# Loads held back until the pooled keys are transposed, and some weight forms on GpSimd, in a pooled-attention and mixture kernel

## The chip, the cores and the metric

The kernel runs on one core of a Trainium2 chip. The metric is the device time of one execution in microseconds; three executions of the kernel before gave 528.2, 528.27 and 527.43, median 528.2. The profiled execution has a span of 526.9 us.

## The reference

Attention with pooled keys and values, followed by a mixture of four two-layer experts:

```python
k_p = k.reshape(B, H, Sp, 8, D).mean(axis=3)        # 576 keys -> 72
v_p = v.reshape(B, H, Sp, 8, D).mean(axis=3)
attn = softmax(q @ k_p.T / sqrt(D))                 # B = 8, H = 8, S = 576, D = 64
x = (attn @ v_p) as [B * S, H * D]                  # 4608 x 512
out = sum over e of p[:, e] * (relu(x @ w1[e]) @ w2[e])   # 4 experts, 512 -> 1024 -> 512
```

with `p` the domain probabilities divided by their sum. All inputs are float32 and are loaded as bf16; the result is float32.

## The kernel before

The tokens are worked in nine chunks of 512: chunk c < 8 holds the first 512 tokens of batch c, and chunk 8 the 64 remaining tokens of all eight batches. A step is one (chunk, expert) pair, 36 in all. In step s TensorE computes the hidden layer of step s and, between its products, the second layer of step s - 1. Most steps multiply by a seven-product scheme (Strassen's, with sums formed ahead of time): `up_seven` and `up_down` form the hidden layer from seven products of 2 x 2 blocks, each accumulated in PSUM; the blocks are sums of halves of x (`forms_of`, tiles `xf`), of w1 (`combine_w1`, written into spare parts of `w1_bf`), of w2 for experts 1 and 2 (`combine_w2`, tile `w2_t`) and of the hidden layer (`sums_of`, tile `h_s`). Chunk 0 is computed in the plain way, and so is the first expert of chunk 1 (`up_plain`); from then on the forms of the weights have to be there.

The attention of batch b = c + 1 is woven into the four steps of chunk c. This is written out by hand: a chunk's plan is a dictionary from a point number to pieces of work, and each pass through `between` or `slot` moves to the next point. In the plan of chunk c, entry n stands at the (2n + 1)st point after the chunk's start, so n runs from 0 to 31, eight to a step. Besides the plan there is a queue `forms_due` of weight and x forms: each `slot` takes one of them, then the pieces of the point. All engines run their own instructions in the order in which the program issues them; between engines only data and buffers hold them.

The pieces of one batch's attention, with their entries before for c > 1:

- `key_parts`: VectorE folds the eight keys of a pool, in two halves of the heads, from the tile `raw` into `kp` (L205, L210, L213).
- `keys` (entry 1; 3 in chunk 1): the SP queue transposes `kp` into `kpT` by DMA (L227).
- `load_v` (entry 2): POOL issues the load of v into the tile `raw` (L91), which holds one batch's k or v and is free once the keys are folded. For batches 1 and 2, v goes into the part of `w2_t` that the w2 forms take later. `load_q` and `load_q_rem` of the next batch come at the same entry (L108, L127).
- `scores` (entries 7 to 10): TensorE multiplies `kpT` and `qT` (L257), ScalarE exponentiates.
- `value_parts` (entries 8 to 11): VectorE folds v into `vp` in the same way (L205, L210, L213).
- `queries` and `load_k` of the next batch (entry 12): the SP queue transposes q (L240), POOL loads k (L91).
- `context` and `turn` (entries 11 to 15): TensorE multiplies exponentials and `vp` (L380), VectorE divides (L361, L362), the SP queue transposes the result into `xT` (L401).

The SP queue carries, in order, all DMA transposes and the output stores (L834). POOL does nothing but issue loads once its constants are made. POOL runs ahead of the others, so a load starts as soon as its buffer is free and the earlier loads of the queue are issued.

Of the kernel before, what the change touches and what calls it, by code (L numbers as in the profile page):

```python
# [13 lines left out]
BF16 = mybir.dt.bfloat16  # L14
# [4 lines left out]
def kernel(  # L19
# [10 lines left out]
    nc = tc.nc  # L30
# [18 lines left out]
    SPLIT = (1, 2)  # L49
# [4 lines left out]
    const = ctx.enter_context(tc.tile_pool(name="const", bufs=1))  # L54
# [124 lines left out]
    state = {}  # L179
# [45 lines left out]
    def keys(b):  # L225
        state[("kpT", b)] = apool.tile([P, H, SPP], BF16, name="kpT", bufs=3)
        nc.sync.dma_start_transpose(  # L227
            out=state[("kpT", b)][:], in_=kp[:].rearrange("j h u d -> j (h u d)")
        )

    def fold_values(b, hs):
        raw = raws[("vraw", b)]
        fold(raw, hs)
        nc.vector.tensor_add(
            out=vps[b % 3][:, hs, 0:D], in0=raw[:, hs, 0, :], in1=raw[:, hs, 1, :]
        )
# [226 lines left out]
    def rem_turn(i):  # L463
        flip(state.pop(("xr", i)), x_rem[:, :, i * P:(i + 1) * P])
# [56 lines left out]
    def attention(c):  # L521

        lo, hi = halves
        b = c + 1
        plan = {}

        def add(n, *what):
            plan.setdefault(n, []).extend(what)

        if c % 2:  # L530
            i = c // 2
            add(18, lambda: rem_queries(i))
            add(23, lambda: rem_scores(i))
            add(26, lambda: rem_context(i))
            add(27, lambda: rem_turn(i))
        if b == B:
            for part in forms_of(B):
                add(31, part)
            return plan
        if c == 1:  # L540
            keyed = 3
            add(0, lambda: queries(b))
            for n, part in enumerate(key_parts(b)):
                add(n, part)
        else:
            keyed = 1
            for n, part in enumerate(key_parts(b)[2:]):
                add(n, part)
        scored, valued, mixed = 7, 8, 11
        add(keyed, lambda: keys(b))  # L550
        if c > 1:
            add(keyed + 1, lambda: load_v(b))
        if b + 1 < B:
            add(keyed + 1, lambda: (load_q(b + 1), load_q_rem(b + 1)))
        for pair in range(NPAIR):
            add(scored + pair, lambda pair=pair: scores(b, pair))
        for n, part in enumerate(value_parts(b)):
            add(valued + n, part)
        if b + 1 < B:
            add(valued + 4, lambda: queries(b + 1), lambda: load_k(b + 1))  # L560
            for n, part in enumerate(key_parts(b + 1)[:2]):
                add(30 + n, part)
        for r in range(NR):
            add(mixed + r, lambda r=r: context(b, r))
            add(mixed + 1 + r, lambda r=r: turn(b, r))
        for n, part in enumerate(forms_of(b)):
            add((20, 21, 28, 29)[n], part)
        return plan
# [4 lines left out]
    A11, A12, A21, A22, S1, S2, S4 = range(7)  # L573
    S3 = A21

    def combine_w1(e):

        w = w1_bf[:, e]
        add, sub = nc.vector.tensor_add, nc.vector.tensor_sub
        return [  # L580
            lambda: add(out=w[:, S1], in0=w[:, A21], in1=w[:, A22]),
            lambda: sub(out=w[:, S2], in0=w[:, S1], in1=w[:, A11]),
            lambda: sub(out=w[:, S4], in0=w[:, A12], in1=w[:, S2]),
            lambda: sub(out=w[:, S3], in0=w[:, A11], in1=w[:, A21]),
        ]
# [21 lines left out]

    def combine_x(c):

        for part in forms_of(c):  # L610
            part()

    def combine_w2(e):

        lo, hi = slice(0, TH), slice(TH, DM)
        b11, b12 = w2_bf[:, e, 4:8, lo], w2_bf[:, e, 4:8, hi]
        b21, b22 = w2_bf[:, e, 0:4, lo], w2_bf[:, e, 0:4, hi]
        t1, t2, t4 = (w2_t[:, SPLIT.index(e), i] for i in range(3))
        sub = nc.vector.tensor_sub
        return [  # L620
            lambda: sub(out=t1, in0=b12, in1=b11),
            lambda: sub(out=t2, in0=b22, in1=t1),
            lambda: sub(out=b12, in0=b22, in1=b12),
            lambda: sub(out=t4, in0=b21, in1=t2),
        ]
# [217 lines left out]
    with tc.manual_schedule(engines={ENG.PE, ENG.DVE, ENG.Activation, ENG.Pool, ENG.SP}):  # L843
        nc.vector.memset(zeros[:], 0.0)
        nc.vector.memset(pool_map[:], 1.0)
        for vp in vps:
            nc.vector.memset(vp[:, :, D:D + 1], float(POOL))
        nc.vector.memset(kp[64:SPP], 0.0)
        for hs in halves:
            load_first(k, "k", hs)  # L850
        nc.gpsimd.affine_select(
            out=pool_map[:], in_=pool_map[:], compare_op=ALU.is_ge, fill=0.0,
            base=0, pattern=[[1, FT], [-POOL, SP]], channel_multiplier=FT,
        )
        nc.gpsimd.affine_select(
            out=pool_map[:], in_=pool_map[:], compare_op=ALU.is_ge, fill=0.0,
            base=POOL - 1, pattern=[[-1, FT], [POOL, SP]], channel_multiplier=-FT,
        )
        for half in range(2):
            load_first_q(half)  # L860
        make_identity(nc, ident[:])
        for hs in halves:
            load_first(v, "v", hs)
        load_w1(0)
        load_w2(0)
        attention_first()
        load_probs()
        load_w1(1)
        load_w1(2)
        load_w2(1)  # L870
        load_w1(3)
        load_k(1)
        load_w2(2)
        load_q(1)
        load_v(1)
        load_w2(3)
        load_q_rem(0)
        load_q_rem(1)

        steps = [(c, e) for c in range(NCH) for e in range(E)]  # L880
        forms_due = deque()
        placed = {}
        at = 0

        def point():
            nonlocal at
            for piece in placed.pop(at, ()):
                piece()
            at += 1

        def slot():
            if forms_due:
                forms_due.popleft()()
            point()

        for s in range(len(steps) + 1):
            live = s < len(steps)
            if live:
                c, e = steps[s]
                if e == 0:  # L900
                    plan = second_attention() if c == 0 else {}
                    if 0 < c < B:
                        plan = {at + 2 * n + 1: what for n, what in attention(c).items()}
                    for n, what in plan.items():
                        placed.setdefault(n, []).extend(what)

            def between(j, n):
                point()
                if s > 0:
                    down(*steps[s - 1], j, n)  # L910
                slot()

            nothing = [lambda: None] * 4
            if s == 1:
                forms_due.extend(nothing + combine_w1(2))
            elif s == 2:
                forms_due.extend(combine_w1(3))
            elif s == 4:
                forms_due.extend(combine_w1(1) + forms_of(1))
            elif s == 5:  # L920
                forms_due.extend(combine_w1(0) + combine_w2(SPLIT[0]) + combine_w2(SPLIT[1]))
            for j in range(2):
                if not live:
                    for n in range(4):
                        between(j, n)
                elif s == 0:
                    for i in range(4):
                        up_half(j, i)
                        if j == 0 and i in (1, 2):
                            turn_here(0, i + 1)  # L930
                        if j == 0 and i == 2:
                            norm_probs()
                            combine_x(0)
                        between(j, i)
                elif s == 1:
                    for n in range(4):
                        between(j, n)
                    for n in range(4):
                        up_plain(c, e, [4 * j + n])
                elif s == E:  # L940
                    for n in range(4):
                        between(j, n)
                        if j:
                            up_plain(c, e, [2 * n, 2 * n + 1])
                elif splits(*steps[s - 1]):
                    up_down(c, e, j, *steps[s - 1])
                else:
                    up_seven(c, e, j, lambda n: between(j, n))
# [30 lines left out]
```

The softmax here doesn't subtract the row's maximum and nothing guards it: scores larger than these inputs give would overflow.

## Time and profile before

| | busy us | share of the span |
|---|---|---|
| PE (matmul) | 506.4 | 96% |
| DVE (VectorE) | 353.0 | 67% |
| ACT (ScalarE) | 267.7 | 51% |
| POOL (GpSimd) | 46.8 | 9% |

| transfers by issue | count | median us to landing |
|---|---|---|
| kpT<-kp, DMA transpose on SP | 6 | 7.0 |
| qT<-q_sb, DMA transpose on SP | 6 | 4.3 |
| raw<-v, load on POOL, 576 KB | 5 | 10.0 |
| q_sb<-q, load on POOL, 512 KB | 7 | 13.5 |

PE is the engine that sets the end. Its idle time and its clock are therefore what counts; the other engines' busy time counts only where PE waits for them. In a line of waits the engine and line that waited stand ahead of the arrow, what ended the wait behind it, and then the total in us, the number of waits and the longest. In a timeline line stand the start, the time, the engine (with q for its queue), line, operation, out<-in and the number of instructions merged; in brackets is the idle time of the engine just before, with what ended it.

### The profile page before, as it was taken

The numbers are of one execution on the slowest core, as the hardware profiler recorded it, in microseconds if no ns is written. First come the engines' busy times: TensorE is split into PE (matmuls) and PEld (weight loads), VectorE is DVE, ScalarE is ACT, GpSimd is POOL, SyncE is SP. The second block draws the span as 40 slices with busy tenths as digits, with TensorE's granted clock in tenths as the row PEclk, the third lists the DMA queues.
The fourth block names the chain that finished last, engine by engine and source line by source line (L and its number), as shares of the span: only waits on it lengthen the run. The fifth ranks groups of instructions, "written<-read, shape, count | busy, mean of one in ns | idle before, by whom it ended". The sixth has DMA issues, their size and how long they took to land.

```text
span 526.9 us, 10142 instructions
## 1 busy us (share of the span) xinstructions
PE 506.4 (96%) x4171; PEld 365.0 (69%) x4171; DVE 353.0 (67%) x657; ACT 267.7 (51%) x467; POOL 46.8 (9%) x66
## 2 busy tenths in 40 slices
PE   8899986899999999999999999999999999999996
PEld 4656542468866885688668866887578768866883
DVE  2435786398867786678767876787687545764574
ACT  3554422645456554655366536554655445544650
POOL 8452101000010001000100010000000000000000
PEclk9899999899999999999999999999999999999999
DMA  9999999340089108830596049603320110011003
GB/s 137 206 206 205 196 150 150 76 80 1 12 157 133 20 1 139 132 49 11 92 155 63 2 78 159 82 12 50 90 40 1 41 52 1 12 40 40 1 1 80
DMA packets 75133, 41.56 MB, mean 79 GB/s; under 512 B 44480, under 2 KB 70464, under 8 KB 75088
## 3 DMA queue, kind: packets, MB, share of 16 engines
q0 software_dynamic: 33744, 22.63, 30.6%
q1 hardware_dynamic: 41344, 18.29, 17.8%
q8 instruction: 32, 0.52, 0.4%
q14 instruction: 13, 0.11, 0.1%
HBM read 45.16 MB, written 9.44 MB: 104 GB/s over the span
## 4 chain that ended last, share of the span: by engine, by line
PE 74%; DVE 11%; DMA 10%; issue 2%; POOL 2%; ACT 1%; DVEq 0%; POOLq 0%; ACTq 0%
PE g_ps L633 33%; PE o_ps L812 20%; PE u_ps L750 16%; DMA w_bf<-in_moe_w_dram 7%; DMA kpT<-kp 4%; DVE acc L756 2%; DVE H_sb L681 2%; PE two L257 2%; PE two L380 1%; DVE acc L826 1%; DVE h_s L696 1%; PE h_ps L651 1%; DVE x_tok L362 1%; POOL w_bf L142 1%; DVE xf L597 1%
## 5 line engine op out<-in xcount | busy, mean ns | idle before, releaser
L633 PEld LDWEIGHTS <-w_bf 128*128 128x128 bf16 x1848 | 176.2, 98 | 47.7 <-issue 9.2
L812 PE MATMUL o_ps<-w_bf,H_sb 128*128 128x512 bf16 x640 | 161.5, 379 | 0.0
L681 DVE CUSTOM_DVE_ANT_0 H_sb<-g_ps,r 128x512 bf16<-128x512 f32 x166 | 114.0, 687 | 65.1 <-ACT r L677 39.8
L633 PE MATMUL g_ps<-xf,w_bf 128*128 128x256 bf16 x1056 | 148.4, 272 | 2.2 <-DVE H_sb L681 1.2
L677 ACT COPY r<-g_ps 128x512 f32<-128x512 f32 x166 | 97.4, 587 | 102.6 <-PE g_ps L633 98.7
L756 DVE SCALAR_TENSOR_TENSOR acc<-u_ps,p_all,acc 128x512 f32<-128x512 f32 (+1 forms) x128 | 77.9, 612 | 44.0 <-ACT u_ps L776 43.3
L633 PE MATMUL g_ps<-xT,w_bf 128*128 128x256 bf16 x696 | 99.9, 273 | 0.3 <-DVE H_sb L681 0.3
L812 PEld LDWEIGHTS <-H_sb 128*128 128x128 bf16 x640 | 62.4, 98 | 45.8
L684 ACT ACTIVATE H_sb<-g_ps 128x512 bf16<-128x512 f32 x98 | 58.4, 596 | 29.3 <-PE g_ps L633 29.3
L750 PEld LDWEIGHTS <-H_sb 128*128 128x128 bf16 x512 | 49.5, 98 | 7.0 <-DVE H_sb L697 1.3
L750 PE MATMUL u_ps<-w_bf,H_sb 128*128 128x256 bf16 x384 | 52.4, 273 | 0.2
L826 DVE SCALAR_TENSOR_TENSOR acc<-o_ps,p_all,acc 128x512 f32<-128x512 f32 x44 | 32.7, 746 | 11.9 <-PE o_ps L812 11.9
L750 PEld LDWEIGHTS <-h_s 128*128 128x128 bf16 x384 | 37.6, 98 | 4.3
L261 ACT ACTIVATE expT<-two 72x1024 bf16<-72x1024 f32 x28 | 28.6, 1020 | 20.3 <-PE two L257 20.3
L750 PE MATMUL u_ps<-w_t,h_s 128*128 128x256 bf16 x256 | 38.4, 273 | 0.0
L762 ACT COPY g_ps<-g_ps 128x512 f32<-128x512 f32 x32 | 18.3, 572 | 27.9 <-PE g_ps L633 27.9
L823 ACT ACTIVATE acc<-o_ps,p_all 128x512 f32<-128x512 f32 x36 | 24.9, 690 | 7.0 <-PE o_ps L812 7.0
L776 ACT COPY u_ps<-u_ps 128x256 f32<-128x256 f32 x32 | 11.4, 357 | 24.0 <-PE u_ps L750 24.0
L362 DVE TENSOR_TENSOR x_tok<-two,inv 128x512 bf16<-128x512 f32 x32 | 22.1, 691 | 1.1
L91 POOL DMA_DIRECT2D raw<-in_v_dram x5 | 4.1, 822 | 210.3 <-DVE kp L213 210.3
L380 PEld LDWEIGHTS <-expT 72*128 72x128 bf16 x256 | 12.2, 98 | 10.6 <-DVE x_tok L362 2.7
L750 PE MATMUL u_ps<-w_t,H_sb 128*128 128x256 bf16 x128 | 19.2, 273 | 0.0
(104 smaller groups left out, 351.9 us busy)
## 6 DMA issues: line engine op xcount, KB each, us to landing
out_dram<-acc SPq DMA_DIRECT2D x32, 256.0 KB, 5.4
w_bf<-in_moe_w_dram POOLq DMA_DIRECT2D x16, 256.0 KB, 9.7
w_bf<-in_moe_w_dram POOLq DMA_DIRECT2D x4, 1024.0 KB, 16.9
raw<-in_k_dram POOLq DMA_DIRECT2D x7, 576.0 KB, 10.0
q_sb<-in_q_dram POOLq DMA_DIRECT2D x7, 512.0 KB, 13.5
raw<-in_v_dram POOLq DMA_DIRECT2D x5, 576.0 KB, 10.0
w_t<-in_v_dram POOLq DMA_DIRECT2D x2, 576.0 KB, 13.1
out_dram<-acc SPq DMA_DIRECT2D x8, 128.0 KB, 2.3
```

What stands on the lines that cost most here:

```text
L261: nc.scalar.activation(out=state[("expT", b)][:, 2 * pair:2 * pair + 2].rearrange("j h r s p -> j s (h r) p"), in_=two[0:SP].rearrange("j ...
L362: nc.vector.tensor_tensor(out=x_tok[:], in0=c_ps[:, :, :, 0:D], in1=inv[:].unsqueeze(3).to_broadcast([P, 2, NPAIR, D]), op=ALU.mult,)
L633: nc.tensor.matmul(bank[:, t, :], lhsT=w1_bf[:, e, block, kc, lo:lo + P], rhs=x[:, kc, :], start=(first and t == 0 and kc == 0), stop=(t = ...
L677: nc.scalar.copy(out=r[:], in_=ps[:])
L681: nc.vector._custom_dve(TENSOR_ADD_SAT, out=out, in0=ps[:], in1=r[:], s0=BIG, s1=0.0)
L684: nc.scalar.activation(out=out, in_=ps[:], func=ACT.Relu)
L750: nc.tensor.matmul(out, lhsT=lhs[0][:, lhs[1] + f, lhs[2]], rhs=rhs[0][:, rhs[1] + f, rhs[2]], start=(start and f == 0), stop=(f == FCH // ...
L756: nc.vector.scalar_tensor_tensor(out=acc, in0=ps, scalar=prob, in1=acc, op0=ALU.mult, op1=ALU.add,)
L762: nc.scalar.copy(out=s[:], in_=g[:])
L812: nc.tensor.matmul(sums[r][:], lhsT=hidden[(c, e)][:, fc, r * P:(r + 1) * P], rhs=w2_bf[:, e, fc, :], start=(fc == 0), stop=(fc == FCH - 1),)
L823: nc.scalar.activation(out=accs[(c, r)][:], in_=o_ps[:], func=ACT.Copy, scale=prob)
L826: nc.vector.scalar_tensor_tensor(out=dst, in0=o_ps[:], scalar=prob, in1=dst, op0=ALU.mult, op1=ALU.add,)
```

## The change

It does three things. A copy of one element from `kpT` on POOL, in front of the loads of v and of the next q, makes POOL wait until the pooled keys of this batch have been transposed; so these loads don't run beside that transpose. In chunk 1 the keys are folded and transposed earlier (entry 1 rather than 3), the values are folded two entries earlier, and the forms of w1 and x are moved behind them. And eight weight forms of 128 x 1024 elements, those of w2 for expert 2 and of w1 for expert 0, run on GpSimd instead of VectorE.

```diff
+    mark = const.tile([1, 1], BF16, name="mark")
+
+    def loads_wait(b):
+        nc.gpsimd.tensor_copy(out=mark[:], in_=state[("kpT", b)][0:1, 0, 0:1])
...
         if c == 1:
-            keyed = 3
+            keyed = 1
             add(0, lambda: queries(b))
             for n, part in enumerate(key_parts(b)):
-                add(n, part)
+                add(n // 2, part)
...
-        scored, valued, mixed = 7, 8, 11
-        add(keyed, lambda: keys(b))
+        scored, valued, mixed = 7, 8 if c > 1 else 6, 11
+        add(keyed, lambda: keys(b), lambda: loads_wait(b))
...
-    def combine_w1(e):
+    def combine_w1(e, engine=nc.vector):
...
-        add, sub = nc.vector.tensor_add, nc.vector.tensor_sub
+        add, sub = engine.tensor_add, engine.tensor_sub
...
     def combine_x(c):
 
-        for part in forms_of(c):
-            part()
-
-    def combine_w2(e):
+        parts = forms_of(c)
+        return [lambda: (parts[0](), parts[1]()), lambda: (parts[2](), parts[3]())]
+
+    def combine_w2(e, engine=nc.vector):
...
-        sub = nc.vector.tensor_sub
+        sub = engine.tensor_sub
...
             elif s == 4:
-                forms_due.extend(combine_w1(1) + forms_of(1))
+                forms_due.extend(nothing[:2] + combine_w1(1) + combine_x(1))
             elif s == 5:
-                forms_due.extend(combine_w1(0) + combine_w2(SPLIT[0]) + combine_w2(SPLIT[1]))
+                forms_due.extend(nothing[:3] + combine_w2(SPLIT[0]))
+                forms_due.extend(combine_w2(SPLIT[1], nc.gpsimd) + combine_w1(0, nc.gpsimd))
```

Steps 4 and 5 are the first two experts of chunk 1. The entry at which k of the next batch is loaded follows `valued`, so in chunk 1 it moves from 12 to 10 as well.

More of the change, by code (lines that the diff above doesn't have):

```diff
@@ L932 @@
                             norm_probs()
-                            combine_x(0)
+                            for part in combine_x(0):
+                                part()
                         between(j, i)
```

## The prediction

> **What bounds the kernel now.** I read the page's slices first, then the waits, the chain of waits, the timeline around the one large hole, and last the landing times of the transfers concerned.
>
> ```profile
> PE   8899986899999999999999999999999999999996
> ...
> PEclk9899999899999999999999999999999999999999
> ```
>
> PE is at 9 tenths almost everywhere, so the end moves only by idle time or slow clock of PE. One slice is the exception after the start: the seventh digit (79 to 92 us) is 6, beside a granted clock of 8 in the next. The waits say on what:
>
> ```profile
> POOL raw L91 <- DVE kp L213: 210.3, 5, 61.6
> ...
> PE two L257 <- DMA kpT<-kp: 6.5, 2, 5.8
> ...
> DVE raw L205 <- DMA raw<-in_v_dram: 3.1, 3, 1.7
> ...
> PE two L380 <- DVE vp L213: 0.9, 1, 0.9
> ```
>
> PE waits 6.5 us in two places for the transposed keys (5.85 in chunk 1, 0.67 in chunk 3, at 207.4 us), and 0.9 for the pooled values. The list has two more facts that matter: POOL issues a v load as soon as the fold of the keys frees the buffer, and VectorE waits three times for that load, so a v load has no slack on VectorE already. The timeline, chunk 1:
>
> ```profile
> 82.10 0.89 POOL L108 DMA_DIRECT2D q_sb<-in_q_dram  x1 [12.08 <-DMA qT<-q_sb]
> ...
> 83.22 1.22 SPq L227 DMA_TRANSPOSE kpT<-kp  x1
> ...
> 83.66 0.84 POOL L91 DMA_DIRECT2D raw<-in_k_dram  x1
> ...
> 93.29 0.64 PE L257 MATMUL two<-qT,kpT 64*72 64x256 bf16 x4 [5.85 <-DMA kpT<-kp]
> ...
> 93.86 3.58 PE L651 MATMUL h_ps<-xT,w_bf 128*128 128x512 bf16 x8
> ```
>
> The keys are pooled at 83.19 (row L213), their transpose is issued at 83.22 and lands 10.02 us later, beside a q load issued 1.1 us before it and a k load issued 0.4 us after. PE had reached the scores at 87.44. After the hole, eight L651 matmuls take 3.58 us where the same eight took 1.89 at 84.69: from 93.29 to 97.25 PE does in 3.96 us what takes 0.34 + 1.73 = 2.07 at full clock, so the hole costs another 1.89.
>
> **What the Trainium skill says.** "TensorE: Matmul & The Clock Gate", What's actually happening: PE falls to half clock after an idle window of about 3.4 us. The trace agrees: the clock record stands at 0.5 from 90.5 to 97.3. "DMA: Bandwidth & Descriptors", Queues, rings and completion order: each of the 16 DMA engines goes round the queues packet by packet, and a transfer is complete only when every engine has posted its increment. The trace agrees: of the kpT transpose issued at 254.97, all but a few of its 256-byte packets are over by 257.5, yet it lands at 261.10, after the loads have begun. "SBUF — State Buffer", Who interferes with whom: a VectorE instruction with two SBUF inputs and a GpSimd instruction that reads SBUF exclude each other for the whole instruction. No run here shows it yet: POOL does no arithmetic in the middle of this kernel.
>
> **The change, part by part.**
>
> *Key parts and keys of chunk 1 two to a point, transposed at its point 1 instead of 3; two empty slots ahead of w1's forms.* VectorE finishes its last relu sum at about 76.5. Two halves of key folding follow at once: per half 0.60 + 0.45 + 0.43 us from start to start (rows L205, L210, L213 at 77 to 83), together 2.95, so kp is ready at 79.45 rather than 83.19. The SP queue is free at 78.6 (qT issue 77.28 + 1.32), and the output stores, which came ahead of kpT, now come behind it. kpT issues near 79.5.
>
> *The gate.* Transposes without loads beside them: 2.4 us for four blocks of 128 columns (xT at 111.26, x_rem at 134.67) and 4.3 for sixteen (qT); eight blocks give about 3.0 by the straight line. So kpT lands at 82.5 to 84, 3.5 to 5 us before PE wants it at 87.44, and the 5.85 goes. With it goes the 1.89 of half clock. Queued behind the gate on POOL are q(3), its remainder and k(3): issue moves from 82.10 to about 83 or 84; qT(3) is issued at 103 and k(3) folded from 140, so this is hidden. The copy itself has no row before: between nothing and the 0.81 to 0.91 us of POOL's DMA issues; I take 0.3. In chunk 3 the 0.67 goes too.
>
> *v, q behind the gate in chunks 2 to 6.* Before, kpT took 6.2, 8.5, 6.1, 6.0 and 7.7 us, and v, issued 0.24 after it, landed 10.2, 10.2, 11.2, 10.0 and 9.2 after kpT's issue. Now v starts at 3.0 + 0.3. Its own time is between 7.1 us (the load at 69.17, nearly alone) and 9.4 (k loads beside transposes). So it lands at 10.4 to 12.7. How late it may be is read in chunk 4:
>
> ```profile
> 266.23 0.69 DVE L205 TENSOR_TENSOR raw<-raw 72x1024 bf16<-72x1024 bf16 x1 [1.74 <-DMA raw<-in_v_dram]
> ...
> 269.00 0.69 DVE L681 CUSTOM_DVE_ANT_0 H_sb<-g_ps,r 128x512 bf16<-128x512 f32 x1 [0.83 <-ACT r L677]
> ...
> 270.78 0.29 DVE L213 TENSOR_TENSOR vp<-raw 72x256 bf16<-72x256 bf16 x1
> ```
>
> v landed 11.16 after the kpT issue; VectorE still had 0.83 us idle before the next sum, and vp was ready at 271.07, just as PE's context matmuls (from 271.01) reached it. So v may land some 12.0 us after the kpT issue before PE waits; the other chunks have the same order. Each of five chunks then loses 0 to 0.7; I take 0.5 in all. q(b+1) lands a little later too, qT and the four xT transposes behind it on SP with it; xT is wanted eight points later (some 15 us), so it is hidden.
>
> *Values of chunk 1 two points earlier.* v(2) has landed at 76.30, so only VectorE's order counts: the 0.91 wait for vp goes.
>
> *Eight forms to GpSimd.* w1 of expert 0 and w2 of expert 2 leave VectorE: 8 x 0.60 = 4.8 us less in the stretch 97 to 124, where VectorE is almost without gaps and PE waited 0.69 and 0.49 for relu sums. On POOL the price is that of "GPSIMD Engine Reference", Elementwise side-by-side: 4497 ns for 2048 fp32 elements, half of it for 1024, 2.25 us each as an estimate; the low bound is its ratio of 1.96 on our 0.68, 1.33. Eight take 11 to 18 us. They may start when v(2) is folded (about 93, since w_t was its buffer) and end by 111 to 115; w2 of expert 2 is wanted when step 7 starts and w1 of expert 0 when step 8 does (130 and 144 before, 7.7 sooner now), so no one waits for the results. Their cost is the port: about nine VectorE instructions with two SBUF inputs fall into these 18 us (four w2 forms of expert 1, four H sums, an xf). If each waits half a POOL instruction, 1.1 us, that is 10 us of VectorE time against the 4.8 saved. Bounds for PE: the 1.2 us of waits gone, or 5 us more, since the H sums stand right before up_down, which reads the second and third of them within 3 us. I take 1.5 lost.
>
> Sum: -5.85 - 1.89 - 0.67 - 0.91 + 0.5 + 1.5 = -7.3; 528.2 - 7.3 = **520.9**.
>
> **The rivals.** *Port lock in full.* The four H sums alternate with POOL forms: 5 us of PE waits in place of 1.5, 524.4; with a half-clock window after it 526. For: VectorE has no gap there. Against: it has 4.8 us less to do. *v too late.* If kpT takes 4 us and v still 10, v lands at 14.3, 2.3 over the limit in four chunks and 1.2 in the last (no q load): 10.4 us in place of 0.5, **530.8, slower**. For: v is the only transfer VectorE waits for. Against: its former 10 us held the transposes and the stalled packets at its start. *kpT(2) not early enough*, because VectorE or the qT ahead of it on the queue holds it: half the hole stays, 524.5.
>
> **How the numbers follow.** Forecast 0.55, port lock 0.22, v late 0.15, kpT late 0.08. The low end is the forecast with neither port nor v cost and the 1.2 us of waits gone: 528.2 - 9.3 - 1.2 = 517.7, less 0.7 of scatter. The high end is the port lock with its slow window, 526.5; v late lies beyond. Faster: the three cases ahead plus a mild form of v late, 0.85; same 0.03; slower 0.12.
>
> **What would show it.** The chunk-1 hole and the 0.5 clock at 90 us gone; kpT landing about 3 us after issue in all chunks; POOL copies right after; L205 of v waiting no more than 2.5 us and PE's L380 without waits; POOL forms near 2.2 us between 93 and 115; VectorE instructions with two SBUF inputs stretched or delayed only there. Wrong if PE shows L380 waits in every chunk, or a hole near 107 to 112.

## The result, and the profile after

| | median us | executions |
|---|---|---|
| before | 528.24 | 527.43 to 528.5 (4) |
| after | 524.97 | 524.13 to 525.83 (4) |

The ratio after to before is 0.9941 with a 95% interval of 0.992 to 0.9961: 3.3 us or 0.6% faster, where 7.3 us were forecast (520.9). In the kernel after, line numbers below the added helper are five higher: L257 is L262, L380 is L385, L681 is L686.

The slices first:

```profile
PE   8898989969999999999999999999999999999996
...
PEclk9999999999999999999999999999999999999999
```

The seventh slice, where PE waited for the keys, is at 9. The low digit is now the ninth (105 to 118 us). The clock is at 9 throughout. The waits (who waited, for what, total, times, longest):

```profile
DVE raw L205 <- DMA raw<-in_v_dram: 13.5, 5, 3.7
...
PE g_ps L638 <- DVE H_sb L686: 3.8, 2, 2.0
...
PE u_ps L755 <- DVE h_s L703: 1.5, 1, 1.5
...
PE two L385 <- DVE vp L213: 1.2, 2, 0.8
```

No line of PE waiting for kpT is left. VectorE waits for v in all five chunks, 13.5 us in place of 3.1, and PE has new waits for relu sums and hidden sums. (One of the two waits for a relu sum, 1.99 us at 46.7 us, lies in the start-up, where this execution had no half clock and the one before had 3.4 us of it at 19 to 22 us; at 62 us the two differ by 0.55.) The timeline of chunk 1:

```profile
80.28 1.22 SPq L227 DMA_TRANSPOSE kpT<-kp  x1
...
83.14 0.40 POOL L234 COPY mark<-kpT 1x1 bf16<-1x1 bf16 x1 [12.57 <-DMA kpT<-kp]
...
83.63 0.90 POOL L108 DMA_DIRECT2D q_sb<-in_q_dram  x1
...
87.92 0.41 PE L262 MATMUL two<-qT,kpT 64*72 64x256 bf16 x4
...
88.26 1.90 PE L656 MATMUL h_ps<-xT,w_bf 128*128 128x512 bf16 x8
```

kpT lands 2.8 us after its issue, almost 5 us before PE wants it, and the eight plain matmuls behind the scores take 1.90 us, not 3.58.

Where the rest went is read by comparing one instruction across kernels: the exponential that follows the scores (row L261, L266 in the kernel after). The table has the difference to the kernel before, in us, at its first instance (the attention of chunk 0, 62.45 us before, a start-up difference), its sixth (the second scores of chunk 1, 98.91), and the first of chunks 2, 3, 4 and 6 (154.16, 208.54, 263.26, 371.62), and at the end of the span (526.92). A difference between two neighbours is what that stretch gained or lost. Each row is one profiled execution, so it shows where time went inside a kernel; which kernel is faster is read from the medians below. (The execution of e2 is the fastest of its six, 1.7 us under their median.)

| kernel | start | 98.9 | 154.2 | 208.5 | 263.3 | 371.6 | end |
|---|---|---|---|---|---|---|---|
| after | +0.55 | -7.28 | -4.04 | -4.78 | -3.79 | -3.80 | -3.32 |
| e1, forms on VectorE | +0.60 | -7.23 | -7.68 | -8.42 | -7.55 | -7.55 | -7.21 |
| e2, no gate | -0.56 | -8.39 | -5.16 | -5.90 | -5.90 | -5.90 | -5.89 |
| e3, before, forms on GpSimd | +0.85 | +0.20 | +4.74 | +4.00 | +4.00 | +4.00 | +4.00 |
| e4, w1 forms after the sums | +0.23 | -7.60 | -8.68 | -9.42 | -8.49 | -8.50 | -8.48 |
| e5, e4 without the gate | +0.26 | -7.57 | -8.63 | -9.37 | -9.37 | -9.37 | -9.33 |
| e6, before, early keys | -0.04 | -7.87 | -7.87 | -8.61 | -8.61 | -8.61 | -8.62 |
| e7, before, gate | +0.23 | -7.30 | -7.29 | -7.86 | -6.78 | -6.78 | -6.60 |
| e8, e1 without the gate | +0.78 | -7.05 | -7.50 | -8.12 | -8.12 | -8.12 | -8.11 |

Row "after": 0.55 lost in the start-up, where the kernels do the same work and these executions differ by up to 1.4 us; 7.83 gained at the hole; 3.24 given back before chunk 2; 0.74 gained in chunk 2 to 3; 0.99 and 0.48 given back in chunk 3 and from chunk 6 on. The sum is -3.3. (A wait costs about 0.16 us more than its idle time: 0.83 cost 0.99, 0.32 cost 0.48. Matmuls in a row overlap in the records, which would explain it; this was not tested.)

The 3.24 lie at 93 to 114 us. POOL and VectorE there, from their timelines:

```profile
95.91 2.12 POOL L627 TENSOR_TENSOR w_t<-w_bf,w_t 128x1024 bf16<-128x1024 bf16 x1
...
110.65 2.56 POOL L589 TENSOR_TENSOR w_bf<-w_bf 128x1024 bf16<-128x1024 bf16 x1
```

```profile
96.01 2.56 DVE L626 TENSOR_TENSOR w_t<-w_bf 128x1024 bf16<-128x1024 bf16 x1
...
106.94 1.77 DVE L701 TENSOR_TENSOR h_s<-H_sb 128x1024 bf16<-128x1024 bf16 x1
108.63 0.68 DVE L686 CUSTOM_DVE_ANT_0 H_sb<-g_ps,r 128x512 bf16<-128x512 f32 x1
109.23 2.00 DVE L702 TENSOR_TENSOR H_sb<-H_sb 128x1024 bf16<-128x1024 bf16 x1
111.16 2.60 DVE L703 TENSOR_TENSOR h_s<-h_s,H_sb 128x1024 bf16<-128x1024 bf16 x1
113.79 0.69 DVE L704 TENSOR_TENSOR h_s<-H_sb,h_s 128x1024 bf16<-128x1024 bf16 x1
```

A hidden sum on VectorE takes 0.69 us when POOL is done (113.79) and 1.77 to 2.60 while a POOL form runs: L626 starts 0.10 us after POOL's L627 and ends 0.54 after it. In the kernel before, the second and third of these sums:

```profile
115.35 0.68 DVE L697 TENSOR_TENSOR H_sb<-H_sb 128x1024 bf16<-128x1024 bf16 x1
115.94 0.68 DVE L698 TENSOR_TENSOR h_s<-h_s,H_sb 128x1024 bf16<-128x1024 bf16 x1
```

PE, in the same place of the kernel after:

```profile
109.36 1.03 PE L638 MATMUL g_ps<-xf,w_bf 128*128 128x256 bf16 x8 [1.77 <-DVE H_sb L686]
111.29 1.05 PE L755 MATMUL u_ps<-w_bf,H_sb 128*128 128x256 bf16 x8 [0.90 <-DVE H_sb L702]
113.82 0.61 PE L755 MATMUL u_ps<-w_t,h_s 128*128 128x256 bf16 x4 [1.48 <-DVE h_s L703]
```

Three waits, 4.15 us, each for a sum or for the relu sum behind one. And the v load, in chunk 3, on VectorE and PE:

```profile
208.66 0.69 DVE L205 TENSOR_TENSOR raw<-raw 72x1024 bf16<-72x1024 bf16 x1 [3.67 <-DMA raw<-in_v_dram]
```

```profile
212.63 0.29 PE L385 MATMUL two<-vp,expT 72*128 72x65 bf16 x4 [0.83 <-DVE vp L213]
```

### The profile page after: what moved, and what is told of

The parts are those of the page before. It is cut to its first block, busy times and chain, and to the rows that moved or that the text cites. A ratio compares the mean times of both kernels' runs of the same rounds, so it can differ in the third digit from the quotient of the medians.

```text
span 523.6 us, 10155 instructions
## 1 busy us (share of the span) xinstructions
PE 504.0 (96%) x4171; PEld 363.5 (69%) x4171; DVE 355.4 (68%) x649; ACT 267.5 (51%) x467; POOL 67.5 (13%) x80
## 4 chain that ended last, share of the span: by engine, by line
PE 71%; DVE 13%; DMA 10%; POOL 2%; issue 2%; ACT 1%; POOLq 0%; ACTq 0%; SPq 0%; DVEq 0%
PE g_ps L638 30%; PE o_ps L817 19%; PE u_ps L755 16%; DMA w_bf<-in_moe_w_dram 5%; DMA raw<-in_v_dram 3%; DVE H_sb L686 3%; DVE acc L761 3%; DMA kpT<-kp 2%; PE h_ps L656 1%; PE two L262 1%; PE two L385 1%; POOL w_bf L142 1%; DVE h_s L701 1%; DVE x_tok L367 1%; DVE H_sb L702 1%
## 5 line engine op out<-in xcount | busy, mean ns | idle before, releaser
L686 DVE CUSTOM_DVE_ANT_0 H_sb<-g_ps,r 128x512 bf16<-128x512 f32 x166 | 113.9, 687 | 48.1 <-ACT r L682 33.3
L831 DVE SCALAR_TENSOR_TENSOR acc<-o_ps,p_all,acc 128x512 f32<-128x512 f32 x44 | 32.7, 746 | 11.3 <-PE o_ps L817 11.3
L266 ACT ACTIVATE expT<-two 72x1024 bf16<-72x1024 f32 x28 | 28.6, 1020 | 13.4 <-PE two L262 13.4
L234 POOL COPY mark<-kpT 1x1 bf16<-1x1 bf16 x6 | 1.3, 218 | 205.9 <-DMA kpT<-kp 205.9
L205 DVE TENSOR_TENSOR raw<-raw 72x1024 bf16<-72x1024 bf16 x22 | 15.0, 681 | 13.5 <-DMA raw<-in_v_dram 13.5
L385 PEld LDWEIGHTS <-expT 72*128 72x128 bf16 x256 | 12.0, 98 | 12.4 <-DVE x_tok L367 4.8
```

The source lines that it names most:

```text
L266: nc.scalar.activation(out=state[("expT", b)][:, 2 * pair:2 * pair + 2].rearrange("j h r s p -> j s (h r) p"), in_=two[0:SP].rearrange("j ...
L686: nc.vector._custom_dve(TENSOR_ADD_SAT, out=out, in0=ps[:], in1=r[:], s0=BIG, s1=0.0)
L831: nc.vector.scalar_tensor_tensor(out=dst, in0=o_ps[:], scalar=prob, in1=dst, op0=ALU.mult, op1=ALU.add,)
```

## The experiments

Two disputes were open. Do the 3.24 us come from GpSimd's work, which shuts VectorE's two-input instructions out of SBUF (the port theory), or from VectorE's new order (the order theory)? And what is the gate worth, the copies on POOL that hold the loads back? Each kernel was timed in five rounds against the kernel before on the same chip (528.3 us for e1 to e4, 527.77 for e5 to e8).

**e1, the forms back on VectorE.**

```diff
-                forms_due.extend(combine_w2(SPLIT[1], nc.gpsimd) + combine_w1(0, nc.gpsimd))
+                forms_due.extend(combine_w2(SPLIT[1]) + combine_w1(0))
```

> The changed kernel with its eight GpSimd forms back on VectorE, in the same places of the queue of forms. Port theory (a GpSimd form and a VectorE instruction with two SBUF inputs exclude each other, which costs PE some 3 us between 98 and 114 us): every two-input VectorE instruction is back at 0.68 us, PE's waits between 98 and 126 us fall from 4.7 us to 1.5 or less, time about 522 us. Order theory (VectorE is late there because the hole that let it catch up is gone and the folds were moved, GpSimd or not): the waits stay at 4 us or grow with the 4.8 us of forms, time 525 us or more.

520.83 us, ratio 0.9872 (0.9853 to 0.9891). PE's waits between 95 and 130 us are 1.8 us in place of 4.85 in the kernel after, and the four sums take 0.68 or 0.69 us. The port theory holds, the order theory falls. The kernel before had 2.27 us of waits there, 1.36 without the 0.91 for vp.

**e2, no gate.**

```diff
-        add(keyed, lambda: keys(b), lambda: loads_wait(b))
+        add(keyed, lambda: keys(b))
```

> The changed kernel without the POOL copies that make the loads wait for kpT. Gate theory (without it the loads hold up the transpose of chunk 1): kpT of chunk 1 takes 7 to 10 us again, PE waits 3 to 6 us at 87 us, time 529 to 532 us. Early-keys theory (in chunk 1 the keys alone, issued at 80.3 us, are done before the next q load can begin, since that load waits for qT, which lands at 82.2): no hole in chunk 1, kpT there under 4 us; in chunks 2 to 6 kpT takes 6 to 8 us again, the 0.7 us wait of chunk 3 comes back, the v waits of 0.83 and 0.32 us go; time 524 to 525 us.

524.46 us, ratio 0.9929 (0.991 to 0.9947), which can't be told from the kernel after by these intervals. The traces say what happens inside: in chunk 1 kpT lands in 2.87 us with no gate at all. The q load waits for qT and is issued at 81.61 us, and none of its packets comes before kpT lands at 82.04. In chunks 2 to 6 it takes 5.1 to 6.3 us again and PE doesn't wait for it, and its waits for vp are gone: the row of e2 stays at -5.90 from chunk 3 on, where the row of the kernel after loses 1.47. So the early-keys theory holds, but for its 0.7 us wait in chunk 3, which did not come back.

**e3, the kernel before with only the forms moved to GpSimd.** The queue of step 5 is the one of the kernel after; `combine_w1` and `combine_w2` take the engine.

```diff
-                forms_due.extend(combine_w1(0) + combine_w2(SPLIT[0]) + combine_w2(SPLIT[1]))
+                forms_due.extend(nothing[:3] + combine_w2(SPLIT[0]))
+                forms_due.extend(combine_w2(SPLIT[1], nc.gpsimd) + combine_w1(0, nc.gpsimd))
```

> The kernel before with only the eight forms moved to GpSimd (queue of step 5 as in the changed kernel), no gate, keys and values where they were. Port theory: GpSimd starts when v is folded at about 106 us and works for some 20 us, beside four w2 forms, eight hidden sums and xf of VectorE, which stretch to 1.2 to 2.6 us each; PE's waits between 105 and 130 us grow from 1.2 to 4 us or more; time 530 to 533 us. Order theory: VectorE has 4.8 us less to do, the waits shrink; time 527 us.

533.64 us, ratio 1.0108 (1.0088 to 1.0128): slower, as the port theory has it and the other can't, and a little above the 530 to 533 expected. PE's idle time at 114 to 121 us is only 3.3 us; the rest of what the stretch lost is clock, which was not expected. A view of busy time in the stretch 114 to 125 us (us, then busy PE, PE loads, VectorE, ScalarE, POOL with instructions, granted clock, DMA share, GB/s):

```profile
114.00:125.00 11.00, 7.69 (x45) 5.17 (x43) 10.97 (x9) 3.05 (x8) 10.84 (x5) 0.69 0.12 24
```

VectorE is busy in 10.97 of 11 us with nine instructions; the kernel before ran 17 in 9.45 us there, at clock 1.00. The record stands at 0.5 from 117.6 to 124.4 us.

**e4, the w1 forms held behind the sums of step 5.**

```diff
+    def sums_wait():
+        nc.gpsimd.tensor_copy(out=mark[:], in_=h_s[0:1, 2, 0, 0:1])
...
-                forms_due.extend(combine_w2(SPLIT[1], nc.gpsimd) + combine_w1(0, nc.gpsimd))
+                forms_due.extend(combine_w2(SPLIT[1], nc.gpsimd) + [sums_wait] + combine_w1(0, nc.gpsimd))
```

> The changed kernel, with a one-element POOL copy of the last hidden sum of step 5 ahead of the four w1 forms, so that they run behind the four sums instead of beside them; nothing else. Port theory: the four sums before up_down take 0.68 us each again, the PE waits of 1.77, 0.90 and 1.48 us at 107 to 114 us go or fall under 1 us in all, the w1 forms run at about 109 to 120 us; time 521.5 to 523 us. Order theory: the waits stay; time 525 us.

520.06 us, ratio 0.9847 (0.983 to 0.9864), below the 521.5 to 523 expected. The same eight forms on the same engine, only four of them 6.5 us later (the first at 109.52 us, not 103.06), and the loss is gone. VectorE, from the timeline:

```profile
106.11 0.68 DVE L704 TENSOR_TENSOR h_s<-H_sb 128x1024 bf16<-128x1024 bf16 x1
106.71 0.68 DVE L689 CUSTOM_DVE_ANT_0 H_sb<-g_ps,r 128x512 bf16<-128x512 f32 x1
107.31 0.68 DVE L705 TENSOR_TENSOR H_sb<-H_sb 128x1024 bf16<-128x1024 bf16 x1
107.91 0.68 DVE L706 TENSOR_TENSOR h_s<-h_s,H_sb 128x1024 bf16<-128x1024 bf16 x1
```

PE's waits between 95 and 130 us are 0.73 us. GpSimd's four w2 forms still run at 93 to 103 us and stretch three of VectorE's (2.56, 1.17 and 1.17 us); that costs PE one wait of 0.36 us. From 98.9 to 154.2 us e4 gains 1.08 us, where e1 gains 0.45: placed like this, the work on GpSimd is worth some 0.6 us in the traces.

**e5, e4 without the gate** (the edit of e2 on e4).

> The changed kernel with the w1 forms on GpSimd behind the hidden sums and without the POOL copies for kpT: both costs of the change taken out, the early keys kept. If the gate costs 1 to 1.5 us in the chunks from 3 on and brings nothing in chunk 1, this is 1 to 2 us below the same kernel with the gate (520.1): 518.5 to 519.5. If the gate is worth something that the single removal hid, 520.5 or more.

519.34 us, ratio 0.9837 (0.9817 to 0.9857), the lowest median of all, and it beats both kernels. In the table it parts from e4 only in chunk 3 and after: -9.37 held to the end, where e4 gives 0.93 back.

**e6, the kernel before with early keys only.**

```diff
-            keyed = 3
+            keyed = 1
...
-                add(n, part)
+                add(n // 2, part)
```

> The kernel before with the keys of chunk 1 folded two parts to an entry and transposed at entry 1; no gate, forms, x forms and values as before. Early-keys theory: kpT of chunk 1 lands in 3 to 4 us, at 84 us, the hole of 5.85 us and the half clock after it (1.9 us) go, nothing else moves: 520 to 521 us. Gate theory (both are needed): the loads still reach the transpose, PE waits 2 us or more at 87 us: 524 us or more.

520.23 us, ratio 0.9852 (0.9838 to 0.9867). Two lines bring more than the whole change: 7.83 us at the hole, nothing given back. kpT of chunk 1 lands in 2.71 us, though the q load is issued 1.15 us after it: its first packets come after kpT has landed.

**e7, the kernel before with the gate only** (`loads_wait` as in the diff of the change, nothing else).

> The kernel before with only the POOL copies that hold the loads until kpT has landed; keys of chunk 1 at entry 3 as before, all forms on VectorE. If the transpose is slow only because of the loads: kpT of chunk 1, issued at 83.2 us, lands at 86 to 87.4 us, just before PE asks for it at 87.4, the hole goes or shrinks below 1 us; v lands later in chunks 2 to 6 and costs 1 to 1.5 us: 521 to 523 us. If its slowness is its own (the output stores ahead of it on SP, the qT transposes): it takes 6 us or more, the hole stays at 2 us or more: 525 us or more.

521.72 us, ratio 0.9878 (0.9858 to 0.9898). kpT of chunk 1, issued at 83.45 us, lands in 4.41 us instead of 10.02, a little later than expected, and the hole shrinks to this:

```profile
87.90 0.41 PE L262 MATMUL two<-qT,kpT 64*72 64x256 bf16 x4 [0.23 <-DMA kpT<-kp]
```

So the loads were what held the transpose up, and either remedy alone fills the hole; the second brings nothing more. PE waits 0.93 us for vp in chunk 3, the price of the gate: the row loses 1.08 there and 0.18 from chunk 6 on.

**e8, e1 without the gate** (the edit of e2 on e1).

> The changed kernel with the forms back on VectorE and without the POOL copies for kpT: early keys, early values and the new order of the forms, nothing of GpSimd. Against the same with the gate (520.8): 1 to 1.5 us less, 519.3 to 520, with no v waits of PE in chunks 3 and 6. Against early keys alone it shows what the earlier values and the reordered forms are worth: 0 to 1 us.

519.53 us, ratio 0.9843 (0.9827 to 0.986). No v waits of PE, as expected. From 98.9 to 154.2 us it gains 0.45 where e6 gains nothing: that is what the earlier values and the reordered forms are worth. By time e4, e5, e6 and e8 can't be told apart; their intervals overlap.

## Why the prediction was right or wrong, point by point

- **The hole of chunk 1: right.** Forecast -5.85 and -1.89 of half clock, together -7.74; measured -7.83 from start-up to the second scores. kpT issued at 80.3 rather than 79.5 and took 2.8 us where 3.0 was drawn from the xT and qT transposes. What the Trainium skill says of the clock in "TensorE: Matmul & The Clock Gate", What's actually happening, fits this hole: with the 5.85 us of idle time the half clock went. It doesn't fit e3 (last section). But the forecast gave the gain to the gate and the early keys together. e6 and e7 show that each does it alone, and e2 that the gate does nothing here once the keys are early.
- **The port: right mechanism, and this is the step that failed, "I take 1.5 lost": the term came to some 4.2.** The durations were well priced: 2.12 us for a POOL form alone against the 2.25 estimated from the Trainium skill's "GPSIMD Engine Reference", Elementwise side-by-side, 18 us of POOL work forecast and 19.5 used (93.7 to 113.2), seven VectorE instructions stretched by 7.7 us in all, 1.1 each, against nine by 1.1. What was wrong is the netting: the 10 us of stretched time were set against the 4.8 us of forms that VectorE no longer does. The three stretched hidden sums (1.09 + 1.32 + 1.92 = 4.33 us more than 0.68 each) stand directly ahead of the matmuls that read them, and PE waited 4.15 us; the time saved on VectorE lay elsewhere, where PE was not waiting. With the 0.91 of vp and the 1.18 of old relu waits gone, the stretch to chunk 2 still lost 3.24 us; the forecast's terms there (-0.91 + 1.5) made 0.59. That is 2.65 of the 4.1 us by which the forecast missed; set apart from the 0.91 gained, the term is 3.24 + 0.91 = 4.15 where 1.5 was taken (the three waits make the same sum by chance: the relu waits that went and the extra cost of each new wait also count). The rival "port lock in full" had 5 us of waits and 524.4, and this is in the main what happened; its half-clock window didn't come in the kernel after. A sign named as that of an error, "a hole near 107 to 112", is there: the three waits lie between 107.6 and 113.8. e1, e3 and e4 show the cause from three sides: no POOL forms, POOL forms without the rest, POOL forms at another time.
- **v behind the gate: right limit, cost undersized.** The rule read from chunk 4 before, v no later than about 12.0 us after the issue of kpT, held in every chunk after: v landed 11.3, 13.1, 12.0, 11.5 and 12.5 us after it, and PE waited where it was clearly later, in chunks 3 and 6, by 0.83 and 0.32 us. Two terms were small: from the landing of kpT to the v issue it takes 0.65 to 0.71 us where 0.3 was taken for the copy, and kpT took 4.2 and 3.9 us in those two chunks instead of 3.0. What sets these two apart is a packet of another DMA queue, q8, which the profile calls instruction. The queues while kpT of chunk 3 is under way (195.47 to 199.7 us; packets, MB, share):

```profile
q1 hardware_dynamic: 953, 0.68, 55.5%
q8 instruction: 1, 0.02, 1.3%
```

It starts at 197.55 us and takes 0.88, and the last four data packets of the transpose come only after a gap from 197.65 to 198.41. In the four kernels with the gate, all nine transposes of kpT with such a packet took 3.2 to 4.4 us and the fifteen others 2.7 to 2.8. Output stores follow kpT in both groups, and in e4 a transpose with the packet and no store before its landing took 3.23. That the packet is the cause was not tested. The stretches lost 0.99 and 0.48 us against 0.5 forecast: 0.97 of the miss.
- **What the gate shifts: right, it is hidden.** Behind the gate the k load is issued within 0.5 us of the q transpose in chunks 2 to 5, and that transpose takes 9.5 to 12.1 us where it took 4.3. Nothing waits for it. The collision was moved to a place with slack and not removed.
- **The 0.67 of chunk 3: gained, but not thanks to the change.** All kernels gain 0.57 to 0.74 there, with the gate or without. In e3, which has neither gate nor early keys, kpT took 5.7 us in that chunk, in e5 and e8 7.6 and 7.9, and PE did not wait; in the profiled execution before it had taken 8.53. So that wait was most likely scatter of one execution, and one profile can't tell such a wait from a lasting one.
- **The wait for vp, 0.91: right.** It is gone in the kernel after and in e8, and stays in e6 and e7, where the values keep their place.
- **The remainder,** 0.55 us, is start-up scatter of the profiled executions; with 0.16 gained above the forecast at the hole and in chunk 3, the terms make 4.0, which is the miss between the two profiled executions.

The forecast had the rule of the Trainium skill's "SBUF — State Buffer", Who interferes with whom, and the trace agrees with it: exclusive, for the whole instruction, and only against VectorE's instructions with two SBUF inputs. The relu sum (one input in PSUM) took 0.68 us beside POOL forms throughout.

## What to carry to other kernels

Work moved to an idle engine is not free if it locks a port: ask not how much time it takes from the busy engine but which instruction of that engine stands in its way, and who waits for that one. Place such work by a data dependency, since an engine without waits runs ahead of its place in the program: a copy of one element moved four forms by 6.5 us and won back 4.3 before chunk 2 (the rows of the kernel after and of e4, each from its own start). When two edits aim at one hole, try each alone; here two lines did all of it, and the gate beside them only cost, 0.9 to 1.5 us in the rows of e4 against e5 and of the kernel after against e2.

## What the runs showed of the hardware that was not expected

- POOL's forms and VectorE's two-input instructions alternate strictly when both have work (from 95.9 us on in the kernel after): POOL's recorded time grows from 2.12 to between 2.45 and 2.57 us, VectorE's instruction ends 0.54 us after POOL's, and POOL's next recorded start lies inside VectorE's instruction. Both engines' recorded times include the wait, so a busy share counts waiting as work.
- In e3 the half clock begins at 117.61 us, when PE has waited 1.78 us for a relu sum and is 0.15 us into its next wait. The kernel after and e2 have the same two waits (1.77 and 0.90 us) at the same distance, with a longer third one behind them, 1.48 us, and keep full clock. The page cited above has the clock fall after an idle window of about 3.4 us; no wait here is that long, so the page's rule doesn't describe e3. Idle time alone does not decide; what does was not tried.
- A transpose by DMA of 80 x 1024 takes 2.7 to 2.9 us from issue to landing when neither a load nor a packet of q8 comes between, 3.2 to 4.4 with a packet of q8 and no load, and 5.1 to 10.0 beside loads.
